# Scores one step earlier and a third buffer for gathered V in a fused block-sparse attention and MoE kernel on one Trainium2 core

## The chip, the cores and the metric

The kernel runs on one core of a Trainium2 chip. A core has five engines that run their own instruction streams and wait for one another through semaphores: TensorE (PE in the profile, with the loading of its weights shown apart as PEld), VectorE (DVE), ScalarE (ACT), GpSimd (POOL) and SyncE (SP, which here only starts transfers). Transfers go through 16 DMA engines. The metric is the device time of one launch in microseconds; smaller is better.

## The reference

Attention over 4 batches, 8 heads, 768 positions of 64 features, in 24 blocks of 32 positions, and then a mixture of experts on its output:

```python
mask = np.abs(blk_i - blk_j) <= 1
mask |= (blk_i == 0) | (blk_j == 0) | (blk_i == 23) | (blk_j == 23)
for qb in range(24):
    for kb in sampled_blocks[qb]:          # 3 blocks per query block, data
        mask[rows(qb), cols(kb)] = True
attn = softmax(where(mask, q @ k.T / 8, -1e9))
x = (attn @ v) as rows of 3072 tokens x 512

logits = x @ w_gate                        # 8 experts
e = argmax(logits); g = softmax(logits)[e]; s = sigmoid(x @ w_output_gate)[e]
out = g * s * (relu(x @ w1[e]) @ w2[e])    # w1 512x1024, w2 1024x512
```

So query blocks 0 and 23 see all keys, and every other query block sees its own block, its two neighbours, blocks 0 and 23 and three sampled ones. Which blocks those are, and which expert a token goes to, is known only at run time.

## The kernel before, in words

**Attention.** It runs in two passes (`bp` 0 and 1), each over two batches. A pass has 52 steps: 8 Dense units for the query blocks 0 and 23, then 11 pairs `i` of query blocks with four Sparse units each, in the order (head group 0, batch 0), (0, 1), (1, 0), (1, 1). Step `u0 = 52*bp + 8 + 4*i` is the first of pair `i`. A unit is scored (S, line 490), its maximum taken by DVE (mx, 497), its exponential by ACT (P, 502), transposed by PE (T, 441), copied out of PSUM (pt, by ACT in line 448 for batch 0, by DVE in 450 for batch 1), multiplied with V (O, 515 for the window's V in `vc`, 522 for the gathered V in `vt`), copied by ACT (ob, 531), and its sums taken by DVE (den, 427, and their reciprocal, 540). S of the two batches of a head group is made together, in 32 interleaved small matmuls, in the even step (`mate`).

**What sets the order.** The program is recorded step by step, and `in_order` pins every engine to the recorded order. In a step the parts of several units are recorded: `pT` of the unit two steps back (`LAGS`), `pS` of the present one, `aH` and `dL` (copies of T), `dM`, `pO` of the unit three steps back, and so on; then come the hooks of the step, pieces of other work put there with `at(step, function, ...)`.

**Rings of buffers.** In PSUM, S has four buffers, O two, and T two. The T buffers are shared with `xp`: a finished pair goes through `turn` (line 677), recorded in step `u0+3` of a later pair, in which PE transposes its x rows into a T buffer, ACT takes the high half out (xT, 679), and DVE the low half (680), for the routing (`lp`, 689 and 690, two steps later). In SBUF there are three K buffers (`kr`), three Q buffers (`qz`), two buffers for the window's V (`vc`) and two for gathered V (`vt`).

**Gathers.** `gather_v` (line 403) issues two indirect transfers on POOL, for the sampled rows of V, two steps ahead of the pair. `gather_k` copies one sampled K block, with a factor, on ACT (383), DVE (381) or POOL (385), and `window_k` (392, 393) copies the window's K on DVE.

**Experts.** Weight pieces arrive in float32 and are split into two float16 halves: ACT makes the high half (`w_h`, 924), DVE the low one (`w_l`, 930). The table `AHEAD` puts the conversions of the first nine pieces into attention's steps; its four numbers are the steps of high, low, high and low, of 512 columns each. The program of the experts begins after step 104. Their rows of x are gathered into the `qz` buffers and three more, `xb`.

Of the kernel before, what the change touches and what calls it, by code (L numbers as in the profile page):

```python
# [28 lines left out]
VW = 65  # L29
RV = 2  # L30
RK = 3
LAGD = (0, 2, 3)
# [7 lines left out]
NE = 2  # L40
# [11 lines left out]
PLAN = 6, (20,)  # L52
AHEAD = ((73, 74, 77, 78), (81, 82, 85, 86), (89, 90, 93, 94), (96, 97, 97, 98), (97, 98, 98, 99), (99, 100, 100, 101),
         (100, 101, 101, 102), (101, 102, 102, 103), (103, 104, 104, 105))
# [36 lines left out]
def tile_kernel(ctx, tc, q, k, v, sampled, wg, wcat, out):  # L91
# [69 lines left out]

    it = sp.tile([128, 128], I32, name="it")
    places = sp.tile([1, NSLOT, 3], I32, name="places")
    ri = sp.tile([128, 1], I32, name="ri")
    vi = sp.tile([128, 2, 12], I32, name="vi")
    pb = sp.tile([128, 4], I32, name="pb")
    qbi = sp.tile([128, NB, 3], I32, name="qbi")
    wi = sp.tile([128, NPAIR, 2], I32, name="wi")
    wf = sp.tile([128, NPAIR, 2], F32, name="wf")
    dup = sp.tile([128, NB, 3], F32, name="dup")  # L170

# [29 lines left out]
    def setup_dup():  # L201

        f = sp.tile([128, NB, 3], F32, name="dupf")
        nc.gpsimd.tensor_copy(f.rearrange("p a c -> p (a c)"), raw[:, :, 0])
        nc.gpsimd.memset(dup[:, :, 0:1], 0.0)
        d = sp.tile([128, NB, 2], F32, name="dupd")
        nc.gpsimd.tensor_tensor(d, f[:, :, 1:3], f[:, :, 0:1].to_broadcast([128, NB, 2]), op=ALU.subtract)
        nc.gpsimd.tensor_tensor(d, d, d, op=ALU.mult)
        nc.gpsimd.tensor_single_scalar(dup[:, :, 1:3], d, 0.5, op=ALU.is_lt)
        d = d[:, :, 0:1]  # L210
        nc.gpsimd.tensor_tensor(d, f[:, :, 1:2], f[:, :, 2:3], op=ALU.subtract)
        nc.gpsimd.tensor_tensor(d, d, d, op=ALU.mult)
        nc.gpsimd.tensor_single_scalar(d, d, 0.5, op=ALU.is_lt)
        nc.gpsimd.tensor_tensor(dup[:, :, 2:3], dup[:, :, 2:3], d, op=ALU.add)

    def setup_const():
        nc.vector.tensor_copy(pcol, ri)
        nc.vector.tensor_single_scalar(ri, ri, 31, op=ALU.bitwise_and)
        iota128 = sp.tile([128, 128], F32, name="iota128")
        nc.vector.tensor_copy(iota128, it)  # L220
# [40 lines left out]
    def setup_blocks():  # L261
        nc.vector.tensor_copy(smp, raw[0:1, :, 0])
        sf = sp.tile([128, NB, 3], F32, name="sf")
        nc.vector.tensor_copy(sf.rearrange("p a c -> p (a c)"), raw[:, :, 0])

        qbf = sp.tile([128, NB, 3], F32, name="qbf")
        nc.vector.tensor_copy(qbf, qbi)
        dd = sp.tile([128, NB, 3], F32, name="dd")
        nc.vector.tensor_sub(dd, sf, qbf)
        bad = sp.tile([128, NB, 3], F32, name="bad")  # L270
        t0 = sp.tile([128, NB, 3], F32, name="t0")
        nc.vector.tensor_single_scalar(bad, sf, 0.5, op=ALU.is_lt)
# [42 lines left out]

    kr = [ring.tile([128, 12, 256], F32, name=f"kr{i}") for i in range(RK)]
    vc = [ring.tile([128, 2, 8, VW], F32, name=f"vc{i}") for i in range(RV)]

    qz = [ring.tile([128, 512], F32, name=f"qz{n}") for n in range(RQ)]
# [80 lines left out]
    def gather_v(bp, i):  # L400
        t = ring.tile([128, 2, 2, 8, VW], F32, tag="vt", name=f"vt{bp}_{i}", bufs=RV)
        for s in range(2):
            nc.gpsimd.indirect_dma_start(  # L403
                t[:, s].rearrange("p b j w -> p (b j w)"), None, vscr[bp],
                bass.IndirectOffsetOnAxis(ap=vidx[:, i, s:s + 1], axis=0))
        vt[bp, i] = t
# [474 lines left out]

    xbuf = qz + [ring.tile([128, 512], F32, name=f"xb{i}") for i in range(3)]

    def load_x(s):
        xgs[s] = (att.tile([128, 512], F32, tag="P", name=f"xg{s}", bufs=6) if s < NE else xbuf[2 * s % 6]).bitcast(F16)
        src = xscr[0:128 * RG[GE][1]] if s < NE else xscr
        nc.gpsimd.indirect_dma_start(xgs[s], None, src, bass.IndirectOffsetOnAxis(ap=tabs[s][:, 1:2], axis=0))  # L887

    def x_t(s):
        t = att.tile([128, 512], F32, tag="P", name=f"xs{s}", bufs=6) if s < NE else xbuf[(2 * s + 1) % 6]  # L890
        t = t.bitcast(F16)
# [111 lines left out]
    def at(n, f, *a):  # L1003
        hooks.setdefault(n, []).append((f, a))

    wide = [ring.tile([128, 2, 1024], F32, tag="vt", name=f"wide{i}", bufs=RV) for i in range(2)]
    wide += [kr[2].rearrange("p a n -> p (a n)").rearrange("p (c n) -> p c n", n=1024)]
# [40 lines left out]
    for bp in range(2):  # L1050
# [6 lines left out]
        for i in range(NPAIR):  # L1057
# [3 lines left out]

            lead = 3 if bp or i > 1 else 0
            for kind, n, ns in KC[bp]:
                at(u0 - n - lead if bp or i != 1 else u0 - min(n, 5), gather_k, bp, i, kind, ns)
            at(u0 - 3 - lead, window_k, bp, i)
            at(u0 - 5 + LAGS[2] if bp or i else 6, window_v, bp, i)
            at(u0 - 5 + LAGS[2] if bp or i > 1 else (8, 12)[i], gather_v, bp, i)
        tiles = [NPAIR] + list(range(NPAIR))
# [42 lines left out]
    for m, un in enumerate(units):  # L1111
        lags = LAGD if isinstance(un, Dense) else LAGS
        le, lt, lo = lags
        d = "0" if isinstance(un, Dense) else ""
        for lag, f in ((lt, "pT"), (0, "pS"), (lt, "aH"), (0, "dM"), (lt, "dL" + d), (lo, "pO"), (lo + 1, "aO"), (lo + 1, "dD"),
                       (le, "aE" + ("0" if le else "")), (lo + 2, "fin"), (lo + 3, "fin2")):
# [147 lines left out]
```

## Time and profile before

| what | value |
|---|---|
| median of 3 runs (lowest to highest) | 623.2 us (621.53 to 624.46) |
| the profiled execution | 622.91 us, span 621.0 us |
| PE busy | 564.4 us, 91% of the span |
| PEld busy | 391.3 us, 63% |
| DVE busy | 473.8 us, 76% |
| ACT busy | 435.5 us, 70% |
| POOL busy | 260.6 us, 42% |
| q1, transfers started by hardware queues | 61004 packets, 87.84 MB, 47.9% of the 16 DMA engines' span |
| q0, transfers started by POOL's software queue | 11744 packets, 37.64 MB, 18.2% |

The span is the time from the first instruction to the last; the 1.91 us between it and the profiled execution's time lie outside. Busy time counts instructions that run, not what an engine does while it waits, starts transfers or branches. In the views of waits, `PE T L441 <- DVE den L540` reads: PE stood before a transpose into T of line 441, and what came last of the things it waited for was DVE's instruction on den in line 540. "issue" means that the profile shows nothing it waited for. In the views by window a number in brackets is a count of instructions.

### The profile page before, as it was taken

To read this page: it belongs to the slowest core of one execution; us is meant where nothing else is said; L and a number is where in the kernel's file an instruction comes from. 1 tells how busy PE (TensorE), PEld (TensorE's weight loads), DVE (VectorE), ACT (ScalarE), POOL (GpSimd) and SP (SyncE) were. 2 spreads that over 40 slices of the span, in tenths; PEclk is the share of its full clock that TensorE was granted. 3 is DMA by queue.
4 is the path that set the end of the run, shared out by engine and by line. 5 is a ranking of instruction groups with operands and counts; after the bars stand their busy time and mean duration, and the time that the engine had idled before them with its cause. 6 is when DMAs were issued, how large, how long until landed. Compare 5 with 4: busy or idle time off the path is not lost. (4 is left out here: it accounts for less than half of the span.)

```text
span 621.0 us, 22116 instructions
## 1 busy us (share of the span) xinstructions
PE 564.4 (91%) x8275; PEld 391.3 (63%) x8275; DVE 473.8 (76%) x934; ACT 435.5 (70%) x834; POOL 260.6 (42%) x324
## 2 busy tenths in 40 slices
PE   6799988989889888888979998999999999999996
PEld 4466655555556555555757776777777777777763
DVE  4587657567657567577689988899898989989891
ACT  1466657656557777677459887887888888788871
POOL 4575758765645766665332131131312122131311
PEclk8899989999889899998699999999999999999999
DMA  8986979795865866559227399359943935823491
GB/s 312 381 260 228 320 250 296 274 283 134 285 141 204 257 210 189 176 159 272 53 64 286 83 292 357 83 145 275 301 119 95 309 76 163 265 63 81 94 295 45
DMA packets 72859, 126.94 MB, mean 204 GB/s; under 512 B 38187, under 2 KB 44459, under 8 KB 72492
## 3 DMA queue, kind: packets, MB, share of 16 engines
q1 hardware_dynamic: 61004, 87.84, 47.9%
q0 software_dynamic: 11744, 37.64, 18.2%
q8 instruction: 67, 1.10, 0.7%
q14 instruction: 44, 0.36, 0.2%
HBM read 183.09 MB, written 20.49 MB: 328 GB/s over the span
## 5 line engine op out<-in xcount | busy, mean ns | idle before, releaser
L930 DVE SCALAR_TENSOR_TENSOR kr<-r,kr 128x1024 f16<-128x1024 f32 (+1 forms) x173 | 184.5, 1110 | 17.2 <-ACT kr L924 16.2
L924 ACT ACTIVATE kr<-r 128x1024 f16<-128x1024 f32 (+1 forms) x173 | 156.4, 960 | 0.8 <-DMA r<-in_wcat_dram 0.8
L941 PEld LDWEIGHTS <-kr 128*128 128x128 f16 x2004 | 125.9, 98 | 46.8 <-issue 9.2
L981 POOL DMA_INDIRECT out_dram<-yo,tab x28 | 29.7, 1059 | 213.2 <-ACT yo L978 191.1
L972 PE MATMUL y<-kr,hh 128*128 128x512 f16 x423 | 114.0, 379 | 0.4 <-DVE hh L959 0.4
L502 ACT ACTIVATE P<-S,mx 128x256 f32<-128x256 f32 x176 | 74.5, 478 | 46.1 <-DVE mx L497 42.4
L941 PE MATMUL h<-xb,kr 128*128 128x128 f16 x1344 | 93.3, 219 | 2.1 <-DMA xb<-qz 2.1
L497 DVE TENSOR_REDUCE mx<-S 128x2 f32<-128x512 f32 x88 | 59.9, 680 | 30.2 <-PE S L490 30.1
L930 DVE SCALAR_TENSOR_TENSOR ws<-r,ws 128x1024 f16<-128x1024 f32 (+1 forms) x60 | 67.8, 1167 | 8.7 <-ACT ws L924 7.1
L403 POOL DMA_INDIRECT vt<-vscr,vidx x44 | 46.8, 1063 | 55.7 <-PE O L522 45.0
L441 PE MATMUL T<-ident,P 128*128 128x128 f32 x352 | 58.7, 291 | 11.1 <-DVE den L540 6.6
L972 PEld LDWEIGHTS <-hh 128*128 128x128 f16 x594 | 50.0, 98 | 25.7 <-DVE hh L959 1.1
L490 PE MATMUL S<-kr,qz 64*32 64x256 f32 x1408 | 59.4, 400 | 4.3 <-issue 3.8
L924 ACT ACTIVATE ws<-r 128x1024 f16<-128x1024 f32 (+1 forms) x60 | 58.1, 1015 | 0.8 <-PE y L972 0.8
L941 PEld LDWEIGHTS <-ws 128*128 128x128 f16 x684 | 44.3, 100 | 16.9 <-issue 6.1
L952 ACT ACTIVATE hh<-h 128x512 f16<-128x512 f32 (+1 forms) x56 | 30.5, 545 | 33.6 <-PE h L941 31.0
L441 PEld LDWEIGHTS T<-ident,P 128*128 128x128 f32 x352 | 38.8, 145 | 18.0 <-issue 14.0
L522 PE MATMUL O<-vt,pt 128*32 128x65 f32 x1408 | 42.0, 229 | 8.6 <-issue 4.6
L515 PEld LDWEIGHTS O<-vc,pt 128*64 128x64 f32 x704 | 28.7, 140 | 31.2 <-issue 20.8
L680 DVE TENSOR_TENSOR xT<-xp,xT 128x512 f16<-128x512 f32 x24 | 16.6, 692 | 39.4 <-ACT xT L679 36.2
L972 PE MATMUL y<-ws,hh 128*128 128x512 f16 x171 | 46.0, 379 | 0.0
L515 PE MATMUL O<-vc,pt 128*64 128x65 f32 x704 | 41.1, 238 | 3.2 <-DVE den L427 1.3
(227 smaller groups left out, 931.1 us busy)
## 6 DMA issues: line engine op xcount, KB each, us to landing
r<-in_wcat_dram SPq DMA_DIRECT2D x240, 512.0 KB
vscr<-vn SPq DMA_DIRECT2D x12, 520.0 KB
qz<-in_q_dram SPq DMA_DIRECT2D x24, 256.0 KB
xscr<-xq SPq DMA_DIRECT2D x48, 128.0 KB
vc<-vscr SPq DMA_DIRECT2D x22, 260.0 KB
kn<-in_k_dram SPq DMA_DIRECT2D x2, 1536.0 KB
vs<-in_v_dram SPq DMA_DIRECT2D x6, 512.0 KB
kn<-in_k_dram SPq DMA_DIRECT2D x6, 512.0 KB
```

The costliest lines, as they stand in the source:

```text
L403: nc.gpsimd.indirect_dma_start(t[:, s].rearrange("p b j w -> p (b j w)"), None, vscr[bp], bass.IndirectOffsetOnAxis(ap=vidx[:, i, s:s + 1] ...
L441: nc.tensor.transpose(pt[:, 128 * c:128 * c + 128], p[:, 128 * c:128 * c + 128], ident)
L490: nc.tensor.matmul(u.s[64 * h2 + 32 * qi:64 * h2 + 32 * qi + 32, hp], t[p, 64 * j + 32 * qi:64 * j + 32 * qi + 32], g[p, 1 - qi:3:1 + qi, ...
L497: nc.vector.tensor_reduce(mx, self.s, axis=AX.X, op=ALU.max, negate=True)
L502: nc.scalar.activation(p[:, 256 * hp:256 * hp + 256], self.s[:, hp], AF.Exp, bias=self.mx[:, hp:hp + 1])
L515: nc.tensor.matmul(o[64 * h2:64 * h2 + 64, hp, 0:VW], w[:, col:col + 64], cv[:, b, 4 * h2 + 2 * hg + hp], start=hp == 0, stop=False)
L522: nc.tensor.matmul(o[64 * h2 + 32 * qi:64 * h2 + 32 * qi + 32, hp, 0:VW], w[:, col:col + 32], av[:, qi, b, 4 * h2 + 2 * hg + hp], start=Fa ...
L924: nc.scalar.activation(w[:, 0, r], piece(n // 8, n % 8)[:, r], AF.Copy, scale=SW)
L930: nc.vector.scalar_tensor_tensor(w[:, 1, r], piece(n // 8, n % 8)[:, r], SW, w[:, 0, r], op0=ALU.mult, op1=ALU.subtract)
L941: nc.tensor.matmul(hps[n // 4][:, 128 * j:128 * j + 128], w[:, hl, 128 * c:128 * c + 128], x[:, c // 2, xl, c % 2], start=cnt == 0, stop=c ...
L952: nc.scalar.activation(hs[g][0], hps[g][:, 0:m], AF.Relu)
L972: nc.tensor.matmul(ys[s], a[:, m], w[:, l, 512:1024], start=n % 8 == 0 and cnt == 0, stop=n % 8 == 7 and cnt == 2)
```

## The change

Four things change, and nothing else: the scores of the Sparse units are recorded one step earlier (`ls = -1`), with the K gathers and window K a step earlier too (`lead`); gathered V gets three buffers, and its gather is recorded at `u0 - 5` in place of `u0 - 2`; the low halves of the first three weight pieces in `AHEAD` move two steps later; and to have room for the third V buffer, the three extra buffers of expert rows become one tile in the ring of the V buffers, while the constants of the setup lie in a K buffer (`kr[1]`) that isn't filled yet.

```diff
+RG_V = 3
-AHEAD = ((73, 74, 77, 78), (81, 82, 85, 86), (89, 90, 93, 94), (96, 97, 97, 98), (97, 98, 98, 99), (99, 100, 100, 101),
+AHEAD = ((73, 76, 77, 80), (81, 84, 85, 88), (89, 92, 93, 96), (96, 97, 97, 98), (97, 98, 98, 99), (99, 100, 100, 101),
...
-    it = sp.tile([128, 128], I32, name="it")
-    qbi = sp.tile([128, NB, 3], I32, name="qbi")
-    dup = sp.tile([128, NB, 3], F32, name="dup")
...
-        f = sp.tile([128, NB, 3], F32, name="dupf")
+        f = early3(4)
...
     kr = [ring.tile([128, 12, 256], F32, name=f"kr{i}") for i in range(RK)]
+    cut = kr[1].rearrange("p a n -> p (a n)")
+
+    def early3(n):
+        return cut[:, 72 * n:72 * n + 72].rearrange("p (a c) -> p a c", c=3)
+
+    it = cut[:, 0:128].bitcast(I32)
+    dup = early3(11)
+    qbi = early3(12).bitcast(I32)
...
     def gather_v(bp, i):
-        t = ring.tile([128, 2, 2, 8, VW], F32, tag="vt", name=f"vt{bp}_{i}", bufs=RV)
+        t = ring.tile([128, 2, 2, 8, VW], F32, tag="vt", name=f"vt{bp}_{i}", bufs=RG_V)
...
-    xbuf = qz + [ring.tile([128, 512], F32, name=f"xb{i}") for i in range(3)]
+    xbufs = []
+
+    def xbuf(n):
+        if not xbufs:
+            xv = ring.tile([128, 4, 512], F32, tag="vt", name="xv", bufs=RG_V)
+            xbufs.extend(qz + [xv[:, i] for i in range(3)])
+        return xbufs[n % 6]
...
-    wide = [ring.tile([128, 2, 1024], F32, tag="vt", name=f"wide{i}", bufs=RV) for i in range(2)]
+    wide = [ring.tile([128, 2, 1024], F32, tag="vt", name=f"wide{i}", bufs=RG_V) for i in range(2)]
...
-            lead = 3 if bp or i > 1 else 0
+            lead = 4 if bp or i > 1 else 1 if i else 0
...
-            at(u0 - 5 + LAGS[2] if bp or i > 1 else (8, 12)[i], gather_v, bp, i)
+            at(u0 - 5 if bp or i > 1 else (8, 10)[i], gather_v, bp, i)
...
+        ls = 0 if isinstance(un, Dense) else -1
-        for lag, f in ((lt, "pT"), (0, "pS"), (lt, "aH"), (0, "dM"), (lt, "dL" + d), (lo, "pO"), (lo + 1, "aO"), (lo + 1, "dD"),
+        for lag, f in ((lt, "pT"), (ls, "pS"), (lt, "aH"), (0, "dM"), (lt, "dL" + d), (lo, "pO"), (lo + 1, "aO"), (lo + 1, "dD"),
```

In the changed file the lines of the attention and the routing stand 8 lower (441 is 449, 490 is 498, 677 is 685), those of the expert weights 14 lower (930 is 944). No engine has more or fewer instructions. How they move, at the places that the prediction speaks of:

**PE, second pass, pair 4.** The names end in pair, batch, head group: `T_1_4_1_0` is the transpose of pass 1, pair 4, batch 1, head group 0. Before, from that transpose on (the rows after these are the rest of the 32 matmuls of S, then O of batch 1):

```order
L441 MATMUL T_1_4_1_0_5283<-ident,P_4_1_0_5178 128x128 x4
L515 MATMUL O_4_0_0_5292<-vc_182,pt_1_4_0_0_5230 64x65 x4
L522 MATMUL O_4_0_0_5292<-vt_4_5000,pt_1_4_0_0_5230 32x65 x8
L677 MATMUL xp_5324<-ident,x_2_5152 128x2x64 x4
L441 MATMUL T_1_4_0_1_5331<-ident,P_4_0_1_5248 128x128 x4
L490 MATMUL S_5_0_0_5336<-kr_181,qz_184 32x256
L490 MATMUL S_5_1_0_5337<-kr_181,qz_184 32x256
```

Now, from the transpose before that one to the first matmuls of S:

```order
L449 MATMUL T_1_4_0_0_5238<-ident,P_4_0_0_5133 128x128 x4
L523 MATMUL O_3_1_1_5247<-vc_180,pt_1_3_1_1_5179 64x65 x4
L530 MATMUL O_3_1_1_5247<-vt_3_4566,pt_1_3_1_1_5179 32x65 x8
L449 MATMUL T_1_4_1_0_5279<-ident,P_4_1_0_5196 128x128 x4
L498 MATMUL S_5_0_0_5284<-kr_178,qz_181 32x256
L498 MATMUL S_5_1_0_5285<-kr_178,qz_181 32x256
```

and from the last matmul of S on:

```order
L498 MATMUL S_5_1_0_5285<-kr_178,qz_181 32x256
L523 MATMUL O_4_0_0_5306<-vc_179,pt_1_4_0_0_5243 64x65 x4
L530 MATMUL O_4_0_0_5306<-vt_4_4818,pt_1_4_0_0_5243 32x65 x8
L685 MATMUL xp_5352<-ident,x_2_5152 128x2x64 x4
L449 MATMUL T_1_4_0_1_5359<-ident,P_4_0_1_5261 128x128 x4
L523 MATMUL O_4_1_0_5370<-vc_179,pt_1_4_1_0_5304 64x65 x4
L530 MATMUL O_4_1_0_5370<-vt_4_4818,pt_1_4_1_0_5304 32x65 x8
L449 MATMUL T_1_4_1_1_5406<-ident,P_4_1_1_5320 128x128 x4
```

S of pair 5 stood behind xp and T of head group 1; it now stands ahead of O and xp, right behind T of head group 0.

**DVE, the same place.** Before, from the maximum of head group 1's first unit to that of the next pair:

```order
L497 TENSOR_REDUCE mx_4_0_1_5232<-S_4_0_1_5212 128x2
L427 TENSOR_SCALAR den_3_0_0_5126<-O_3_0_1_5163 128x2
L392 TENSOR_SCALAR kr_179<-kn_1061 128x256
L393 TENSOR_SCALAR kr_179<-kn_1061 128x768
L930 SCALAR_TENSOR_TENSOR ws_4949<-r_3611,ws_4949 128x512
L497 TENSOR_REDUCE mx_4_1_1_5288<-S_4_1_1_5213 128x2
L450 COPY pt_1_4_1_0_5290<-T_1_4_1_0_5283 128x512
L427 TENSOR_SCALAR den_3_1_0_5181<-O_3_1_1_5234 128x2
L540 RECIPROCAL den_3_0_0_5126<-den_3_0_0_5126 128x4
L680 TENSOR_TENSOR xT_5323<-xp_5324,xT_5323 128x2x256
```

Now, from window K on:

```order
L400 TENSOR_SCALAR kr_176<-kn_1075 128x256
L401 TENSOR_SCALAR kr_176<-kn_1075 128x768
L702 TENSOR_REDUCE lsum<-lp_5226 128x16
L505 TENSOR_REDUCE mx_4_0_1_5245<-S_4_0_1_5159 128x2
L435 TENSOR_SCALAR den_3_0_0_5136<-O_3_0_1_5181 128x2
L505 TENSOR_REDUCE mx_4_1_1_5302<-S_4_1_1_5160 128x2
L458 COPY pt_1_4_1_0_5304<-T_1_4_1_0_5279 128x512
L435 TENSOR_SCALAR den_3_1_0_5199<-O_3_1_1_5247 128x2
L548 RECIPROCAL den_3_0_0_5136<-den_3_0_0_5136 128x4
L688 TENSOR_TENSOR xT_5351<-xp_5352,xT_5351 128x2x256
```

Window K and the weight's low half stood between the two maxima, ahead of the copy of T; window K now stands ahead of both maxima, and the low half (not among these rows) after the xT.

**POOL, first pass, the gather for pair 10.** Before:

```order
L431 TENSOR_TENSOR x_7_3128<-ob_7_0_0_2866,den_7_0_0_2871 128x256
L658 TENSOR_TENSOR xq_3102<-x_6_2897,xq_3102 128x2x256
L431 TENSOR_TENSOR x_7_3128<-ob_7_1_0_2921,den_7_1_0_2926 128x256
L403 DMA vt_10_3226<-vscr_78,vidx 128x1040 x2
L780 DMA table<-vals,place 25600x4
```

Now:

```order
L439 TENSOR_TENSOR x_6_2897<-ob_6_1_0_2686,den_6_1_0_2691 128x256
L357 COPY vn_1141<-vs_5_2630 128x16x64
L411 DMA vt_10_3072<-vscr_78,vidx 128x1040 x2
L788 DMA table<-vals,place 25600x4
L439 TENSOR_TENSOR x_7_3117<-ob_7_0_0_2877,den_7_0_0_2882 128x256
```

The two gathers stand ahead of the x rows of pair 7, behind which they stood before; on POOL nothing else moves there.

More of the change, by code (lines that the diff above doesn't have):

```diff
@@ L201, in setup_dup @@
     def setup_dup():
-        f = sp.tile([128, NB, 3], F32, name="dupf")
+        f = early3(4)
         nc.gpsimd.tensor_copy(f.rearrange("p a c -> p (a c)"), raw[:, :, 0])
         nc.gpsimd.memset(dup[:, :, 0:1], 0.0)
-        d = sp.tile([128, NB, 2], F32, name="dupd")
+        d = early3(5)[:, :, 0:2]
         nc.gpsimd.tensor_tensor(d, f[:, :, 1:3], f[:, :, 0:1].to_broadcast([128, NB, 2]), op=ALU.subtract)
@@ L218, in setup_const @@
         nc.vector.tensor_single_scalar(ri, ri, 31, op=ALU.bitwise_and)
-        iota128 = sp.tile([128, 128], F32, name="iota128")
+        iota128 = cut[:, 128:256]
         nc.vector.tensor_copy(iota128, it)
@@ L262, in setup_blocks @@
         nc.vector.tensor_copy(smp, raw[0:1, :, 0])
-        sf = sp.tile([128, NB, 3], F32, name="sf")
+        sf = early3(6)
         nc.vector.tensor_copy(sf.rearrange("p a c -> p (a c)"), raw[:, :, 0])
-        qbf = sp.tile([128, NB, 3], F32, name="qbf")
+        qbf = early3(7)
         nc.vector.tensor_copy(qbf, qbi)
-        dd = sp.tile([128, NB, 3], F32, name="dd")
+        dd = early3(8)
         nc.vector.tensor_sub(dd, sf, qbf)
-        bad = sp.tile([128, NB, 3], F32, name="bad")
-        t0 = sp.tile([128, NB, 3], F32, name="t0")
+        bad = early3(9)
+        t0 = early3(10)
         nc.vector.tensor_single_scalar(bad, sf, 0.5, op=ALU.is_lt)
@@ L879, in load_w @@
         nc.sync.dma_start(piece(s, j), src, cond=chg)
-    xbuf = qz + [ring.tile([128, 512], F32, name=f"xb{i}") for i in range(3)]
+    xbufs = []
[4 more added lines that the diff above has]
+        return xbufs[n % 6]
     def load_x(s):
-        xgs[s] = (att.tile([128, 512], F32, tag="P", name=f"xg{s}", bufs=6) if s < NE else xbuf[2 * s % 6]).bitcast(F16)
+        xgs[s] = (att.tile([128, 512], F32, tag="P", name=f"xg{s}", bufs=6) if s < NE else xbuf(2 * s)).bitcast(F16)
         src = xscr[0:128 * RG[GE][1]] if s < NE else xscr
@@ L889, in x_t @@
     def x_t(s):
-        t = att.tile([128, 512], F32, tag="P", name=f"xs{s}", bufs=6) if s < NE else xbuf[(2 * s + 1) % 6]
+        t = att.tile([128, 512], F32, tag="P", name=f"xs{s}", bufs=6) if s < NE else xbuf(2 * s + 1)
         t = t.bitcast(F16)
```

## The prediction

> **What bounds the kernel now.** The page's first part comes first, to see which engine is near its limit over the whole span.
>
> ```profile
> PE 564.4 (91%) x8275; PEld 391.3 (63%) x8275; DVE 473.8 (76%) x934; ACT 435.5 (70%) x834; POOL 260.6 (42%) x324
> ```
>
> TensorE (PE) is busy for 91%, so at most 56.6 us of the 621.0 are its idle time; a change that leaves its instructions alone can win only from that and from a low clock. Where the idle time lies, the windows by stage tell: the middles of the two attention passes (first and third row), what joins them (second), the last routing (fourth), the experts (fifth). Behind each stretch stand its length and the busy time of PE, PEld, DVE, ACT and POOL, then granted clock, DMA share and GB/s.
>
> ```profile
> 35.91:136.83 100.92, 89.55 (x1880) 59.77 (x1879) 69.54 (x216) 65.97 (x180) 69.91 (x92) 0.98 0.85 274
> 136.83:185.43 48.60, 42.57 (x716) 27.95 (x715) 31.86 (x97) 28.52 (x76) 26.22 (x36) 0.93 0.72 195
> 185.43:278.78 93.35, 80.16 (x1715) 53.24 (x1714) 62.31 (x192) 67.43 (x183) 60.55 (x75) 0.98 0.64 199
> 278.78:326.00 47.22, 39.04 (x551) 28.68 (x551) 35.09 (x94) 26.89 (x53) 19.59 (x19) 0.82 0.47 132
> 326.00:621.00 295.00, 286.54 (x3129) 204.19 (x3126) 254.29 (x261) 234.28 (x314) 66.19 (x54) 1.00 0.62 180
> ```
>
> The experts keep PE busy for 286.54 of 295.00; the change moves nothing there but buffers, so they only shift with the attention's end. In the first and third stretch (10 and 9 query pairs) PE idles 11.37 and 13.19 us. One period of a pair, undisturbed and with a stall, in the same columns:
>
> ```profile
> 106.26:115.02 8.76, 8.24 (x189) 5.71 (x188) 6.15 (x17) 6.30 (x18) 7.00 (x9) 1.00 1.02 376
> 257.47:268.25 10.78, 9.54 (x190) 5.94 (x189) 6.29 (x17) 7.46 (x21) 7.40 (x10) 1.00 0.59 179
> ```
>
> A pair can pass in 8.76 us; the mean is 10.09 in the first stretch (100.92/10) and 10.37 in the third (93.35/9). What PE and its neighbours wait for, from the view of waits between 36 and 300 us (total, times, longest):
>
> ```profile
> PE T L441 <- DVE den L540: 6.6, 10, 1.7
> PE O L522 <- issue: 4.6, 7, 1.6
> PE O L522 <- DMA vt<-vscr,vidx: 3.9, 2, 2.7
> PE S L490 <- issue: 3.8, 6, 1.4
> PE T1d L441 <- DVE xT L680: 3.9, 2, 2.0
> POOL vt L403 <- PE O L522: 45.0, 18, 3.7
> DVE xT L680 <- ACT xT L679: 35.7, 21, 3.8
> ACT xT L679 <- PE T L441: 12.1, 11, 2.9
> ACT xT L679 <- PE xp L677: 6.6, 6, 2.8
> L441 PE MATMUL T<-ident,P 128*128 128x128 f32 x352 | 58.7, 291 | 11.1 <-DVE den L540 6.6 <-issue 2.3 <-DVE mx L497 1.3
> ```
>
> Two waits of PE can be touched by the change: 11.1 us ahead of the transposes T (the last row, from the groups by form between 40 and 300 us, holds all their releasers) and 3.9 us on gathered V. The waits ended by "issue" before S and O, and those of the Dense units (T1d), belong to work that isn't moved.
>
> **The T stall.** One of the ten, PE first, then DVE, then ACT:
>
> ```profile
> 264.91 0.66 PE L441 MATMUL T<-ident,P 128*128 128x128 f32 x4
> 265.50 0.45 PE L515 MATMUL O<-vc,pt 128*64 128x65 f32 x8
> 266.25 0.66 PE L677 MATMUL xp<-ident,x 128*128 128x128 f32 x4
> 267.69 0.63 PE L441 MATMUL T<-ident,P 128*128 128x128 f32 x4 [0.79 <-DVE den L540]
> 268.25 1.09 PE L490 MATMUL S<-kr,qz 64*32 64x256 f32 x32
> 269.27 0.45 PE L515 MATMUL O<-vc,pt 128*64 128x65 f32 x8
> 265.19 0.56 DVE L393 TENSOR_SCALAR kr<-kn 128x768 f32<-128x768 f32 x1
> 265.66 0.69 DVE L930 SCALAR_TENSOR_TENSOR ws<-r,ws 128x512 f16<-128x512 f32 x1
> 266.86 0.68 DVE L450 COPY pt<-T 128x512 f32<-128x512 f32 x1
> 269.08 0.69 DVE L680 TENSOR_TENSOR xT<-xp,xT 128x512 f16<-128x512 f32 x1 [1.39 <-ACT xT L679]
> 267.71 0.42 ACT L383 ACTIVATE kr<-kn 128x256 f32 x1
> ```
>
> T has two PSUM buffers, shared with xp. The T of 267.69 takes the buffer that the T of 264.91 filled; DVE empties it only from 266.86 to 267.54, having first done window K (L393) and the low half of a weight (L930). What PE has between these two T is O, 0.75 us (265.50 to 266.25), and xp, 0.66: not enough. The profile names den because it came last on DVE.
>
> **Scores a step sooner.** S of a pair goes between the first T and that O. Its price on PE is the same 1.02 us (268.25 to 269.27), but the cover of the DVE eviction grows from 1.41 to 2.43 us. Here T started 0.79 us late, and S alone gives 1.02. Three of the weight pieces that are converted during attention also lose their low half (0.69) from its place ahead of the eviction: it runs two steps later. I count the whole of the T stalls as gone except the part that isn't on a T buffer emptied by L450: of 11.1 I take 10, bounds 5 (only half fit in the added 1.02 and the rest move on) and 11.1. S itself needs its K sooner: the K gathers and window K move a step with it, the same number of instructions on DVE, ACT and POOL, so their slack to S stays. S has four PSUM buffers; a step sooner, it asks for those whose exponentials stood three steps back and now stand two back, still over one step of 2.2 us (8.76/4) away: nothing. Only the first pair of a pass keeps its gathers where they were, with S one step nearer: 0 to 2.2 us; I take 0, since the Dense units fill PE ahead of it.
>
> **What the cover was taken from.** xp takes the other T buffer; the T after next needs it back, after ACT's xT and then DVE's. An undisturbed case, PE and ACT, and one where xT is late:
>
> ```profile
> 105.24 0.66 PE L677 MATMUL xp<-ident,x 128*128 128x128 f32 x4
> 105.93 0.59 ACT L679 CAST xT<-xp 128x512 f16<-128x512 f32 x1 [1.02 <-PE xp L677]
> 124.63 0.38 PE L677 MATMUL xp<-ident,x 128*128 128x128 f32 x2
> 126.58 0.59 ACT L679 CAST xT<-xp 128x512 f16<-128x512 f32 x1 [1.25 <-PE T L441]
> ```
>
> Before, PE had T 0.56 (267.69 to 268.25), S 1.02 and O 0.75 between xp's end and that T: 2.33 us. Now S is gone from there: 1.31. The chain that must fit is 0.03 (105.90 to 105.93) + 0.59 + 0.69 + a handover of 0.03, or 1.34 us when ACT starts at once. So every lateness of ACT now shows on PE. In the late row it is 1.57 us (126.58 less 125.01), but eleven of these waits are recorded as ended by the T behind xp, not by xp: they go with the T stall, which leaves. What stays is ACT's own work: a K gather of 0.42 us (L383) now issues in the step of xp in the first pass as well, where ACT stood idle for 1.02. I take 0.25 us, rather more than half of it, for each of 20 pairs (the last of each pass has no S behind it): **+5 us**; bounds 0 (row of 105.93) and 1.57 x 20 = 31.
>
> **The third V buffer.** The gather of a pair writes a buffer that the pair two back still reads, so POOL stands 45.0 us in 18 waits, and the data can come late:
>
> ```profile
> 81.34 0.30 PE L522 MATMUL O<-vt,pt 128*32 128x65 f32 x2
> 84.32 0.43 PE L522 MATMUL O<-vt,pt 128*32 128x65 f32 x14 [2.69 <-DMA vt<-vscr,vidx]
> 80.74 1.35 POOL L403 DMA_INDIRECT vt<-vscr,vidx  x1 [1.49 <-PE O L522]
> 82.39 0.94 POOL L403 DMA_INDIRECT vt<-vscr,vidx  x1 [0.30 <-issue]
> 85.10:88.40 3.30, 3.30 (x43) 0.50 1.02 402
> 88.50:91.90 3.40, 3.40 (x96) 1.00 0.70 271
> ```
>
> With three buffers and the issue three steps sooner (6.6 us), the slot's last reader ends a step before the issue, so both gathers, 1.35 and 0.94 us of POOL, leave without a wait; behind them stand K gathers, x and xq, which come sooner too. **-3.9 us**, bounds 0 (if the transfer only waits elsewhere: the DMA share is 1.02 at 85 us) and -3.9. After the gap of 2.69 us the granted clock was 0.50 for 3.30 us (43 instructions, against 96 in the 3.40 after it; the columns are length, PE busy, clock, DMA share, GB/s): half of it, 1.65 us, goes as well, bounds 0 and -1.65.
>
> [...]
>
> **Buffers that change address.** Expert rows in a slot of the V ring and setup constants in a K buffer add no instruction. The slot's last gathered V is long read when the first row comes, and the constants' readers end before that K buffer is filled: 0. If that cover were gone, one wait at the start or at the experts' start, at most one period of 8.76 us.
>
> **Sum.** The profiled execution took 622.91 us, of which 621.0 is the span; the median is 623.2, 0.05% off, so no correction. 622.91 - 10 - 3.9 - 1.65 + 5 = **612.4**, forecast **612 us**. Its own range, with T between -5 and -11.1 and xT between 0 and 8 (0.4 each), is 605 to 619.
>
> **Rivals.**
> 1. The T stall only changes place: xT is late by another 0.5 us a pair, 20 x 0.5 = 10, as much as T gains. Only V and clock stay: 622.9 - 5.6 + 5 = 622 us. For it: DVE xT waited 35.7 us for ACT's, in all 21 waits. Against it: those waits were hidden, and many follow a stalled T.
> 2. Slower: ACT reaches xT late by the mean of its recorded waits, (12.1 + 6.6)/17 = 1.1 us, in every pair, and each now holds the T of step u0+5: +22 against -15.5, 629 us; with 1.57 each, 639. It decides from 15.5/20 = 0.78 us a pair. For it: ACT's step now begins with a gather. Against it: at 105.93, with T behind xp unhindered, ACT started 0.03 after xp.
> 3. Much better: every pair takes the 8.76 us of the undisturbed one: 10 x 1.33 + 9 x 1.61 = 27.8, so 595 us. For it: DVE, ACT and POOL are busy for 7.00 at most in that period. Against it: the "issue" waits (4.6 and 3.8) and the Dense units stay, and PE was busy for 9.54 in the stalled period.
> 4. The change doesn't do what it says: a scheduler might put S back. The order of the instructions shows it moved; no chance of its own.
>
> **How the numbers follow.** Forecast 0.55, rival 1 0.20, rival 2 0.13, rival 3 0.12. A difference of 0.5% (3.1 us) is about what a measurement of this kernel can tell from none. Faster is the forecast and rival 3, 0.67; the same is rival 1, 0.20; slower is rival 2, 0.13. The range goes from rival 3's 595 to just short of rival 2's 629: 595 to 628 leaves out half of rival 3, more than half of rival 2 and little else.
>
> **What would show it.** Right: no wait of T for den over 0.3 us between 36 and 300 us; POOL's wait before V under 5 us; no wait of O on a V transfer, and no clock of 0.50 near 85 us; mean periods near 9.7 us in both passes (10.2 less 10.5/20); the experts as long as before. Wrong: the transposes T waiting as long as before, now ended by DVE xT, with ACT's xT starting over 0.8 us after xp (rivals 1 and 2); or a new wait at the first pair of a pass. A longer last stretch would refute the zero for the buffers.

## The result, and the profile after

The changed kernel took 643.79 us (median of four runs, 641.56 to 648.35); the kernel before took 623.83 us on the same chip (621.53 to 624.80). The ratio is 1.0335, 95% interval 1.0267 to 1.0402. The forecast was 612 us, so even the sign was wrong here. Medians are of all runs of a kernel; ratios leave out runs in a slower state. The profiled execution took 641.56 us, 18.65 more than the one before.

The waits of the changed kernel between 36 and 300 us (total, times, longest), and from its page the groups of transposes, scores and the two halves of O (count, busy us, mean ns, idle us ahead of them and what ended it):

```profile
PE O L530 <- issue: 22.3, 39, 1.2
POOL vt L411 <- PE O L530: 30.4, 15, 3.7
ACT xT L687 <- PE xp L685: 34.4, 19, 4.3
...
L530 PE MATMUL O<-vt,pt 128*32 128x65 f32 x1408 | 51.0, 232 | 22.3 <-issue 22.3
...
L449 PE MATMUL T<-ident,P 128*128 128x128 f32 x352 | 58.3, 289 | 2.7 <-issue 1.4
...
L498 PE MATMUL S<-kr,qz 64*32 64x256 f32 x1408 | 52.5, 391 | 2.7 <-issue 1.4
...
L523 PE MATMUL O<-vc,pt 128*64 128x65 f32 x704 | 41.4, 239 | 5.8 <-DVE den L435 4.0
```

The same half of O before (from the groups by form, 40 to 300 us) and S (from the page of before), which the prediction didn't show:

```profile
L522 PE MATMUL O<-vt,pt 128*32 128x65 f32 x1408 | 42.0, 229 | 8.6 <-issue 4.6 <-DMA vt<-vscr,vidx 3.9
...
L490 PE MATMUL S<-kr,qz 64*32 64x256 f32 x1408 | 59.4, 400 | 4.3 <-issue 3.8
```

The row of T fell from 11.1 us of idle time to 2.7, and the wait for gathered V (3.9) is gone. In their place stands a wait with no releaser, 22.3 us in 39 pieces, inside the half of O that reads gathered V: with its busy time, which such pieces stretch, that group went from 50.6 to 73.3 us. S went the other way, from 63.7 to 55.2 us with its idle time. One pair, PE, then POOL and ACT:

```profile
84.31 1.09 PE L498 MATMUL S<-kr,qz 64*32 64x256 f32 x32
85.33 0.45 PE L523 MATMUL O<-vc,pt 128*64 128x65 f32 x8
85.72 0.24 PE L530 MATMUL O<-vt,pt 128*32 128x65 f32 x1
86.17 0.31 PE L530 MATMUL O<-vt,pt 128*32 128x65 f32 x3 [0.21 <-issue]
86.89 0.48 PE L530 MATMUL O<-vt,pt 128*32 128x65 f32 x12 [0.41 <-issue]
87.31 0.66 PE L685 MATMUL xp<-ident,x 128*128 128x128 f32 x4
...
84.09 1.01 POOL L411 DMA_INDIRECT vt<-vscr,vidx  x1 [0.93 <-PE O L530]
85.41 0.94 POOL L411 DMA_INDIRECT vt<-vscr,vidx  x1 [0.30 <-issue]
88.00 0.59 ACT L687 CAST xT<-xp 128x512 f16<-128x512 f32 x1 [1.02 <-PE xp L685]
```

Sixteen matmuls that take 0.4 us at a stretch are handed out in three portions over 1.6 us (85.72 to 87.31). It happens in the first O of a pair, the one between S and xp, beside POOL's two gathers, which begin as soon as the last O of the step before ends (here 0.29 us behind it, 84.09 against 83.80). Where POOL scatters to the expert table right behind the gathers, it lasts up to 3.4 us (254.77 to 258.19). In what follows a first O is beside two gathers when it begins between the start of the first and the end of the second (36 to 300 us), and broken when two of its matmuls start more than 0.3 us apart. Here 15 of 15 were broken; from their first matmul to xp they took 29.4 us more together than at the 0.75 us of an unbroken one. In six of the 15 no packet of the queues that the page calls "instruction" was on its way, so a late load of instructions isn't seen as the cause.

Where the 18.5 us of span came from, by the stretches of the prediction (same columns; here they end at the first x tile that PE turns for the experts, 325.03 us before and 339.33 now):

```profile
35.20:136.91 101.71, 88.06 (x1878) 60.15 (x1878) 67.63 (x206) 64.87 (x176) 68.79 (x92) 1.00 0.86 281
136.91:190.21 53.30, 42.98 (x719) 27.82 (x718) 35.19 (x102) 29.98 (x80) 28.61 (x38) 0.97 0.70 178
190.21:289.49 99.28, 84.66 (x1712) 57.35 (x1711) 63.26 (x187) 64.96 (x178) 58.65 (x71) 0.93 0.62 186
289.49:339.33 49.84, 37.49 (x566) 27.23 (x565) 38.85 (x108) 29.52 (x60) 19.03 (x18) 0.90 0.45 108
339.33:639.50 300.17, 290.98 (x3143) 207.16 (x3143) 254.05 (x261) 234.17 (x314) 67.24 (x54) 0.98 0.62 179
...
203.20:210.00 6.80, 6.39 (x74) 0.50 0.89 224
...
339.70:343.10 3.40, 3.40 (x27) 0.50 1.04 370
401.20:404.60 3.40, 3.40 (x16) 0.50 0.77 291
```

First pass +0.8 us, the stretch between the passes +4.7, second pass +5.9, last routing +3.6 (46.25 before, from 278.78 to 325.03), experts +4.2 (295.97 before), and the start 0.7 less. The sixth row is a stretch at half clock in the second pass. Most of the experts' share is two more of them (last two rows; half of 6.8 is 3.4 us), the first of them right behind the wait for that x tile. So 10.7 of the 18.5 us lie ahead of the last routing. In the two passes (+6.7) PE gained on T, on V and on S, and lost more in O. What the stretch between the passes and the last routing lost wasn't taken apart.

### The profile page after: what moved, and what is told of

Same layout as the page of the kernel before. It is cut to its first block, busy times and chain, and to the rows that moved or that the text cites. A ratio compares the mean times of both kernels' runs of the same rounds, so it can differ in the third digit from the quotient of the medians.

```text
span 639.5 us, 22127 instructions
## 1 busy us (share of the span) xinstructions
PE 569.5 (89%) x8275; PEld 396.1 (62%) x8275; DVE 479.3 (75%) x934; ACT 435.4 (68%) x834; POOL 260.1 (41%) x324
## 5 line engine op out<-in xcount | busy, mean ns | idle before, releaser
L944 DVE SCALAR_TENSOR_TENSOR kr<-r,kr 128x1024 f16<-128x1024 f32 (+1 forms) x173 | 184.4, 1109 | 17.3 <-ACT kr L938 15.5
L955 PE MATMUL h<-xv,kr 128*128 128x128 f16 x1344 | 94.3, 220 | 3.2 <-DMA xv<-qz 2.9
L944 DVE SCALAR_TENSOR_TENSOR ws<-r,ws 128x1024 f16<-128x1024 f32 (+1 forms) x60 | 71.8, 1233 | 9.8 <-ACT ws L938 8.3
L530 PE MATMUL O<-vt,pt 128*32 128x65 f32 x1408 | 51.0, 232 | 22.3 <-issue 22.3
L411 POOL DMA_INDIRECT vt<-vscr,vidx x44 | 43.0, 976 | 40.9 <-PE O L530 30.4
L498 PE MATMUL S<-kr,qz 64*32 64x256 f32 x1408 | 52.5, 391 | 2.7 <-issue 1.4
L966 ACT ACTIVATE hh<-h 128x512 f16<-128x512 f32 (+1 forms) x56 | 30.4, 543 | 35.2 <-PE h L955 31.5
L530 PEld LDWEIGHTS O<-vt,pt 128*32 128x32 f32 x1408 | 30.5, 112 | 34.3 <-issue 27.8
```

Source lines behind the costliest of these rows:

```text
L411: nc.gpsimd.indirect_dma_start(t[:, s].rearrange("p b j w -> p (b j w)"), None, vscr[bp], bass.IndirectOffsetOnAxis(ap=vidx[:, i, s:s + 1] ...
L498: nc.tensor.matmul(u.s[64 * h2 + 32 * qi:64 * h2 + 32 * qi + 32, hp], t[p, 64 * j + 32 * qi:64 * j + 32 * qi + 32], g[p, 1 - qi:3:1 + qi, ...
L530: nc.tensor.matmul(o[64 * h2 + 32 * qi:64 * h2 + 32 * qi + 32, hp, 0:VW], w[:, col:col + 32], av[:, qi, b, 4 * h2 + 2 * hg + hp], start=Fa ...
L944: nc.vector.scalar_tensor_tensor(w[:, 1, r], piece(n // 8, n % 8)[:, r], SW, w[:, 0, r], op0=ALU.mult, op1=ALU.subtract)
L955: nc.tensor.matmul(hps[n // 4][:, 128 * j:128 * j + 128], w[:, hl, 128 * c:128 * c + 128], x[:, c // 2, xl, c % 2], start=cnt == 0, stop=c ...
L966: nc.scalar.activation(hs[g][0], hps[g][:, 0:m], AF.Relu)
```

## The experiments

One thing must be known to read the numbers: the runs lie in seven groups, each on one chip (six of these are known to be different chips; that of the first isn't on record). The median of the kernel before is about 620 to 624 us in three groups (623.8, 619.8, 622.8) and about 613 in the other four (613.0, 613.0, 614.3, 613.0), though single runs of the two kinds overlap. Ratios are always against before on the same chip. That the two kinds differ in just this wait was found only late.

**Which part costs it.** Scores alone, in the kernel before:

```diff
-((lt, "pT"), (0, "pS"), ...
+((lt, "pT"), (0 if isinstance(un, Dense) else -1, "pS"), ...
-            lead = 3 if bp or i > 1 else 0
+            lead = 4 if bp or i > 1 else 1 if i else 0
```

> The kernel before with the scores and the K gathers one step sooner, two V buffers, V gathered at u0-2 as before. In the changed kernel no T waits for DVE any more, but the matmuls of O with gathered V stand still for 22.3 us in 39 waits with no releaser, each beginning beside POOL's second gather. Theory A (the gathers hold PE up wherever they fall, and the change moved them beside O): this kernel loses the T stalls and keeps what it has on V, so 612 to 620 us, and no new waits in O before the gathers. Theory B (the new order of PE's work is at fault: S and O stand back to back, and PE is not given its small instructions fast enough): as slow as the changed kernel, 640 us or more, with 15 to 22 us of waits inside O.

and the third V buffer with the gathers three steps sooner alone (the changed kernel with `ls = 0`, the old `lead` and the old `AHEAD`):

> The changed kernel with its third V buffer and the gathers at u0-5, but the scores, the K gathers and the weights' low halves back in their old places. Theory A: the gathers still begin as soon as the buffer's last reader ends, so PE stands still beside them too: 630 us or more, with waits of PE beside most gathers. Theory B: no new waits in O, the V waits of 3.9 us gone: 617 to 621 us.

Measured on one chip of the 620 kind: scores alone 640.26 us, ratio 1.0344 (1.0268 to 1.0420); gathers alone 621.97 us, 1.0003 (0.9950 to 1.0056). From the waits of PE (36 to 320 us), two rows of the first and two of the second, then S in the page of the second:

```profile
PE O L522 <- issue: 23.5, 46, 1.2
PE T L441 <- DVE den L540: 1.3, 1, 1.3
```

```profile
PE T L449 <- DVE den L548: 7.8, 11, 1.4
PE O L530 <- issue: 2.3, 4, 0.8
...
L498 PE MATMUL S<-kr,qz 64*32 64x256 f32 x1408 | 62.1, 383 | 5.8 <-issue 4.6
```

The whole loss comes with the scores, and so does the whole end of the T stall. As it was expected, theory B (PE isn't given its small instructions fast enough in the new order) stood, and A in its plain form (gathers cost the same wherever they fall) fell: with gathers at much the same moments and the old order, O hardly waits. But S pays there: 67.9 us with its idle time, against 63.7 in the kernel before, about as much as the wait for V had cost (3.9). In sum the third buffer neither gains nor costs.

**Are the gathers needed for it?** The changed kernel with no V gathers for pairs 3 to 8, and with copies of the same size by SP in their place, which parts the bytes that land from POOL's own instructions:

```diff
     def gather_v(bp, i):
+        if 3 <= i < 9:
+            vt[bp, i] = vt[bp, i % 3]
+            return
```

```diff
         for s in range(2):
-            nc.gpsimd.indirect_dma_start(...)
+            if 3 <= i < 9:
+                nc.sync.dma_start(t[:, s]..., vscr[bp][128 * s:128 * s + 128, :])
+            else:
+                nc.gpsimd.indirect_dma_start(...)
```

> The changed kernel; for pairs 3 to 8 of each pass V is not gathered, and O reads the V that pairs 0 to 2 of the pass (of the first pair of the pass, for its residue) have left, so this part of the attention is left out of what is right. Theory A: the waits inside O disappear for these 12 pairs, whose periods fall to about 8.8 to 9.3 us, and the time to 625 us or less. Theory B: the waits stay, and the time stays within 1% of 642 us.

> The changed kernel; for pairs 3 to 8 of each pass SP copies the same number of rows and bytes into the V buffer, from consecutive rows in place of the sampled ones, so these pairs work on other V. [...] Theory B: the waits stay.

Both kernels work on other V than the right one in these pairs. Measured, on the same chip: 631.49 and 631.18 us, one run each, against 640.26 with all gathers (scores alone) and 619.78 before: neither theory's number (625 or less, or within 1% of 642). Three periods of the first kernel beside which POOL gathers nothing, and two beside which it does; then one of each of the second:

```profile
67.53:75.60 8.07, 8.07 (x189) 5.63 (x189) 5.97 (x17) 6.46 (x19) 5.09 (x7) 1.00 0.92 273
75.60:83.84 8.24, 8.16 (x190) 5.62 (x189) 6.69 (x18) 6.36 (x19) 5.16 (x7) 1.00 0.62 190
83.84:91.91 8.07, 8.07 (x189) 5.63 (x188) 6.55 (x22) 6.75 (x18) 4.78 (x7) 1.00 0.76 234
110.31:121.19 10.88, 9.10 (x190) 6.06 (x189) 6.64 (x17) 6.25 (x18) 8.18 (x11) 1.00 0.55 176
121.19:133.73 12.54, 10.57 (x189) 6.96 (x188) 6.40 (x22) 6.18 (x16) 6.11 (x7) 0.86 0.81 235
```

```profile
67.70:76.28 8.58, 8.32 (x189) 5.77 (x188) 6.33 (x17) 7.04 (x20) 5.41 (x7) 1.00 0.86 268
113.79:126.04 12.25, 10.45 (x190) 7.20 (x189) 6.79 (x17) 6.38 (x17) 8.15 (x11) 0.86 0.64 233
```

Without POOL's gathers PE is busy to the last tenth (8.07 of 8.07), and a pair is faster than the 8.76 us of the best one before. The two rows with gathers are late pairs, which have scatters to the expert table beside them too; the early pairs of scores alone, by the starts of their first O's, take 9.5 us. Beside two gathers 4 of 4 first O's are broken in either kernel, elsewhere 1 of 14 without V transfers and 4 of 14 with SP's copies (one of these beside POOL's gathers of expert rows). So on this kind of chip both are needed, the new order and POOL's indirect transfers, and for the broken O's it is not mainly the bytes that land. What the bytes cost otherwise stays open: with copies the totals are alike, but single pairs take 8.58, 9.38 and 8.98 us. That the total stayed over 625 us fits the gathers that are left, those of 10 of the 22 pairs.

**Other moments for the gathers.** Four kernels, on a chip of the 613 kind. Pulled apart:

```diff
-            at(u0 - 5 if bp or i > 1 else (8, 10)[i], gather_v, bp, i)
+            at(u0 - 3 if bp or i > 1 else (8, 10)[i], gather_v, bp, i, (0,))
+            at(u0 - 2 if bp or i > 1 else (8, 11)[i], gather_v, bp, i, (1,))
-                        at(t0 + t5 + 1 + (4 if g < 4 ...
+                        at(t0 + t5 + 1 + (g < 4) + (4 if g < 4 ...
```

> The changed kernel with its POOL transfers pulled apart: the first V gather of a pair at u0-3, the second at u0-2, with an x row between them, and the scatters to the expert table a step later, behind K gathers. Starvation theory: from the first indirect transfer on POOL, PE still runs 85 to 90 instructions (1.7 us where S follows T) and then gets a few every 0.7 us until about 0.9 us after the last one. One transfer alone is 1.0 + 0.9 = 1.9 us, so each costs at most 0.2 us, not 1.5 to 3: waits inside O of 22.3 us fall below 8 us, and the time to 612 to 625 us. Rival (what hurts is where PE's order puts S, and the gathers only show it): 635 us or more.

the same in the old order (with `ls = 0`, the old `lead` and `AHEAD`):

> As the run with the POOL transfers pulled apart, but with the scores, the K gathers and the weights' low halves in their old places: the third V buffer and the spread transfers alone. Starvation theory: before, the wait of T for DVE falls into the time in which PE would be starved, so the two cover each other, and the T waits stay when the transfers are pulled apart: 610 to 620 us, T waits of 8 us or more. If T's waits had been starvation and not DVE, they go too: below 612 us with T waits under 4 us.

every gather issued a second time for pairs 3 to 8:

> The changed kernel; for pairs 3 to 8 of each pass every V gather is issued twice, with the same data. Starvation theory: the run of indirect transfers is 2.6 us longer for 12 pairs, and PE is starved for as much longer: periods of 11.5 to 14 us for these pairs, 20 to 31 us in all, about 665 us, in waits of 0.7 us at a time that move on to xp, T and the next O. If only the first gather or the V buffer's release matters: 650 us or less.

and both gathers at u0-2 again (`at(u0 - 5 + LAGS[2] if bp or i > 1 else (8, 12)[i], gather_v, bp, i)`), with three buffers:

> The changed kernel with three V buffers, but the gathers recorded at u0-2 again. Their buffer has been free for a step or more, so they leave when POOL comes to them, behind x rows, not at the end of an O. Starvation theory: the waits fall 85 to 90 PE instructions behind the first gather, on whatever stands there, still 1 to 3 us a pair: 630 to 645 us. If it is the coincidence with the buffer's release that hurts: 620 us or less.

Measured: apart 611.44 us, ratio 0.9977 (0.9938 to 1.0015); apart in the old order 610.21, 0.9954 (0.9920 to 0.9988); twice 738.97 (expected about 665), one run; at u0-2 608.83 against 613.04, one run. I took the first as proof that pulling apart had helped. It was none: at u0-2 POOL runs two gathers in a row again, T, O, T, S and a first O (88 matmuls) pass beside one such pair of gathers without a gap, and O waits for 6.3 us in all. These 6.3 us are 4 waits, each beside a gather or within 0.9 us behind one, so this kind of chip isn't quite free of them. The doubled gathers failed as a dose, since the second one waits for the first to land (7.16 us in one case), so the V of a pair comes late and PE waits for other things. The run in the old order shows the T stalls undiminished:

```profile
PE T L450 <- DVE den L549: 15.5, 17, 1.7
PE O L531 <- issue: 2.7, 3, 1.3
```

That speaks for the prediction's reading of them, as DVE's lateness in emptying the T buffer.

**Same moment, another instruction waits.** POOL writes one column of the new buffer twice ahead of the gathers, so that these writes wait for PE and not the gathers; or it writes the whole buffer, and the gathers come 2 us later; or the gathers stand at u0-4:

```diff
         t = ring.tile([128, 2, 2, 8, VW], F32, tag="vt", ...)
+        nc.gpsimd.memset(t[:, 0, 0, 0, 0:1], 0.0)
+        nc.gpsimd.memset(t[:, 1, 0, 0, 0:1], 0.0)
```

> The changed kernel; ahead of the two V gathers POOL writes one column of the new V buffer twice, so it is these short writes that wait for the last O of the old pair, and the gathers only follow them, at nearly the same moment as before. Wait theory (PE is held up because the gather instruction itself waits for PE): no waits inside the first O of a pair, 3% faster than the changed kernel's 1.0335 of before. Coincidence theory (what counts is that both gathers run beside T, S and the first O of a pair, so beside PE's densest stretch of small instructions): 1.3 to 2.9 us in the first O of most pairs, ratio to before 1.025 to 1.04.

> As the run with the short writes, but POOL writes the whole V buffer ahead of the gathers, which so begin about 2 us later, beside the first O, xp and T and not beside S. Coincidence theory: the waits move away from the first O's start by as much: to the end of O, to xp, T or the next O, and are smaller where PE has fewer instructions there; ratio to before 1.00 to 1.02. Wait theory: as the run with the short writes. If the waits come at a fixed PE instruction whatever the gathers do, they stay in the first O.

> The changed kernel with the V gathers one step later, at u0-4, behind POOL's K gather of that step: their buffer is free by then, so they do not begin with the end of an O. Coincidence theory: the share of gathers that fall beside the first O decides, ratio between 0.99 and 1.02. Wait theory: no waits inside O, ratio 0.985 to 1.0, as with the gathers at u0-2.

> The kernel with the gathers at u0-2 again (one look gave 608.83 against 613.04 us of before), timed in five rounds: with few waits inside the first O and few of T for DVE it should be faster than before by 0.5 to 1.5%. If the one look was luck: ratio 1.00 or more.

Measured, on another chip of the 613 kind: short writes 606.88 us against 613.04, one run; whole buffer 633.15, one run; at u0-4 608.04, ratio 0.9893 (0.9847 to 0.9938); at u0-2 609.96, 0.9887 (0.9819 to 0.9955). With the short writes and, in many pairs, at u0-4 the gathers lie as in the changed kernel, from 1.5 or 1.6 us ahead of the gathered half of the first O to 0.6 or 0.8 us behind its start; but beside two gathers 12 of 14 first O's, and 9 of 9, ran unbroken. That fits neither of the two theories. In the run with the whole buffer other waits are long: window K took DVE longer (1295 ns for the smaller copy in the mean, 717 in the run with the short writes), and S waited 9.1 us for DVE's lsum.

**The chip.** What was left in common was that every run with the new order and few such waits had been on a chip of the 613 kind. So the changed kernel, the kernel before and the short writes ran together on one more chip, and the changed kernel and the spread gathers on yet another:

> The changed kernel itself, on the chip that the next two runs share. The kernel before has taken 623.8, 619.8 and 613.0 us on the chips so far, and every run without waits inside the first O was on a chip of the 613 kind. Chip theory (the waits inside O belong to a chip or to how the program is loaded there, and the kernel runs without them elsewhere): on a 613 chip the ratio to before is 0.985 to 1.00, with under 5 us of waits inside O. Kernel theory (the waits belong to the changed kernel's order of gathers everywhere): ratio 1.025 to 1.04 with some 20 us of waits inside O.

> The kernel before, for a profile of it on this chip. Chip theory: on a 613 chip its waits ended by 'issue' before S and inside O (8.4 us on the first chip) are under 3 us, while T still waits for DVE. Kernel theory: they are as on the first chip.

> The run with two short writes ahead of the gathers, on the same chip as the changed kernel. Kernel theory: 3% faster than it, with no waits inside O. Chip theory: the same time as the changed kernel within 1%, whichever kind of chip this is.

> The changed kernel and the run with its POOL transfers pulled apart, on one more chip. On two chips where the kernel before takes about 620 to 624 us the changed kernel is 3% slower, and the short writes ahead of the gathers change nothing there (644 us); on two chips where it takes 613 us no run has waits inside O. If the kind of chip decides: on a 613 chip 0.985 to 1.00 with under 5 us of waits inside O, on a 620 chip 1.025 to 1.04 with some 20 us. If the changed kernel is slow everywhere: 1.025 to 1.04 on either.

> As the earlier run with the POOL transfers pulled apart (0.9977 on a 613 chip). If two gathers in a row beside T, S and the first O are the cause on 620 chips, pulling them apart takes most of the loss away there: 0.99 to 1.01. If any gather beside small matmuls costs the same there, wherever it stands: 1.02 or more. On a 613 chip: 0.99 to 1.00 as before.

> The run with the POOL transfers pulled apart, once more, hoping for a chip of the 620 kind, where the changed kernel is 3% slower and no version with single gathers has run. If the run of two gathers beside T, S and the first O is what costs there: ratio 0.99 to 1.01, under 8 us of waits inside O. If every gather costs the same wherever it stands: 1.02 or more, with waits of 0.7 us on O, T and S. On a 613 chip: 0.99 to 1.00 again, which leaves this open.

The first chip was of the 620 kind: changed kernel 642.52 us against 622.79, ratio 1.0314 (1.0268 to 1.0360); before 621.39, one run (with "issue" waits of 2.2 us on S and 1.9 in the gathered half of O, where the first chip had 3.8 and 4.6); short writes 644.12, one run. The second was of the 613 kind: changed kernel 606.00 against 614.29, **0.9888 (0.9798 to 0.9979)**; spread 609.30, 0.9943 (0.9904 to 0.9983). The last was also of the 613 kind: spread 611.13, 0.9973 (0.9933 to 1.0012). The changed kernel on the first of these chips, the short writes on it, and the changed kernel on the second:

```profile
PE O L530 <- issue: 23.9, 39, 1.4
```

```profile
PE O L532 <- issue: 20.1, 42, 0.6
```

```profile
PE O L523 <- DVE den L435: 7.2, 8, 1.8
PE T L449 <- DVE den L548: 3.5, 3, 1.7
PE O L530 <- issue: 3.1, 3, 1.6
...
80.32 1.09 PE L498 MATMUL S<-kr,qz 64*32 64x256 f32 x32
81.34 0.45 PE L523 MATMUL O<-vc,pt 128*64 128x65 f32 x8
81.73 0.44 PE L530 MATMUL O<-vt,pt 128*32 128x65 f32 x16
82.09 0.66 PE L685 MATMUL xp<-ident,x 128*128 128x128 f32 x4
...
80.11 1.00 POOL L411 DMA_INDIRECT vt<-vscr,vidx  x1 [1.99 <-PE O L530]
81.42 0.94 POOL L411 DMA_INDIRECT vt<-vscr,vidx  x1 [0.31 <-issue]
```

The same program, the same pair, the gathers again 1.62 us ahead of the half of O that reads them and as long as before: sixteen matmuls in one portion, 0.36 us to xp, where the chip of the first profile took 1.59. Of the first O's beside two gathers 1 of 12 was broken on this chip, 14 of 14 on the one of the 620 kind; with the short writes 15 of 15 on the chip of the 620 kind, 2 of 14 on one of the 613 kind. The mean granted clock hardly differs (0.969 here, 0.963 and 0.955 on the others). Chip theory stands, kernel theory falls as a rule for all chips. Every chip whose number is known appears in one group of runs only, so the chip itself isn't told apart from whatever else the runs of a group may share.

What this doesn't settle: why chips differ, how POOL's transfers hold up PE, and whether spreading the gathers helps on the 620 kind, since all three runs of it were on the other. Nor was a version found that beats the kernel before on both kinds. On the 613 kind the changed kernel, the gathers at u0-4 and at u0-2 are alike, 1.1% faster than before (intervals from 0.2 to 2.0%); on the 620 kind the best complete kernels are the one before and the gathers alone.

## Why the prediction was wrong

- **The T stall (-10).** The mechanism was right, the size nearly: 11.1 us went to 2.7 on the first chip (-8.4), though DVE's den now holds up the window's half of O for 4.0 us, where it was 1.3. On the 613 kind more of it stands there (10.0 us ahead of that half of O, 7.2 of it ended by den, in the page of that run).
- **V waits and clock (-3.9, -1.65).** The wait for V is gone, and the first pass has its full clock (1.00). But the half clock came back elsewhere: 6.8 us at 0.50 from 203.2 us on, and twice 3.4 us in the experts.
- **xT (+5).** Too dear: it measured nothing. No T of a Sparse unit waits for DVE's xT between 36 and 300 us, and ACT starts it 0.03 us after xp ends in the quoted row (87.31 + 0.66, then 88.00). The rivals that rested on a late xT, the slower one among them, named the wrong mechanism; that one of them pointed to a slower kernel was luck.
- **The POOL waits.** Expected under 5 us, measured 30.4: the gathers stand three steps sooner and still wait for the end of an O, since POOL runs that far ahead. That this wait costs nothing by itself is argued, not shown; it sets the gathers right behind that O.
- **Its own range.** From the bounds that the prediction gives for it (T -5 to -11.1, xT 0 to 8) it is 606 to 620, not 605 to 619. Nothing hangs on it.
- **The step that failed** is the sentence that "the waits ended by 'issue' before S and O [...] belong to work that isn't moved". They did move with the order. Before, PE had T and O beside the gathers (4 and 24 small matmuls), then xp and a T that had to wait; now S stands between T and O, and makes 60 small matmuls ahead of xp of those 28. The cost, 20 to 24 us of waits in the gathered half of O on chips of the 620 kind, stands in no term of the sum. The trace of before showed such a place, in S:

```profile
115.02 0.69 PE L490 MATMUL S<-kr,qz 64*32 64x256 f32 x11
116.08 2.21 PE L490 MATMUL S<-kr,qz 64*32 64x256 f32 x21 [0.36 <-issue]
...
114.36 0.95 POOL L403 DMA_INDIRECT vt<-vscr,vidx  x1 [0.30 <-issue]
116.12 1.04 POOL L780 DMA_INDIRECT table<-vals,place  x1 [0.17 <-issue]
```

S takes 3.2 us (115.02 to the next O at 118.22) where others take 1.02, waits for nothing, and POOL's transfers run at the same time. Most of this is in S's busy time and little in its waits; of the 3.8 us of "issue" waits on S two, 2.6 us together, end more than 4 us behind POOL's last transfer, so not beside it. To set the places of long S against POOL's transfers would have put a price beside the gain of 15.5 us, as a slower rival: 2.2 us a pair at most, or 44 for 20 pairs, an estimate from this one row.

The waits of O before (4.6 us) are weaker evidence. Two rows of one pair, and the second of them as it stands in the later profile of the kernel before on a chip of the 620 kind:

```profile
103.31 0.30 PE L522 MATMUL O<-vt,pt 128*32 128x65 f32 x2
104.88 0.43 PE L522 MATMUL O<-vt,pt 128*32 128x65 f32 x14 [1.27 <-issue]
...
106.50 0.43 PE L522 MATMUL O<-vt,pt 128*32 128x65 f32 x14 [1.30 <-DMA vt<-vscr,vidx]
```

The third matmul of this half is the first that reads the pair's second V transfer. Three of the seven waits, 3.1 us, end right there, as the wait for V at 84.32 in the prediction does, and none with the third buffer alone. So they are more likely waits for V that the profile didn't name.

On a chip that hardly has the cost the changed kernel gained about 6.9 us by the ratio (0.0112 x 614.29), where 11 were forecast. No trace of the kernel before was taken on such a chip, so which terms of the sum made this gain isn't shown.

## What to carry to other kernels

A wait with no releaser needn't belong to the work it stands before (here 22.3 us in O, beside POOL's gathers): see which transfers and engines run beside it, and price it for every place that the change moves there. Look at what its first matmul reads, too, since it can be a wait that the profile didn't name (here more likely than not 3.1 of 4.6 us). Filling PE's stall with other work can remove the stall, and with it the slack in which something else was hidden: on the first chip T's idle time fell from 11.1 to 2.7 us, and that of the gathered half of O rose from 8.6 to 22.3. A gain or loss of 1 to 3% is measured on more than one chip before it is believed: here the same program was 3.3% slower on one and 1.1% faster on another.

## What the runs showed of the hardware that was not expected

- The same program on different chips: beside POOL's two gathers the first O of a pair was broken in 15 of 15 and 14 of 14 cases in two groups of runs, in 18 of 18 in a third (with the scores alone), and in 1 of 12 in a fourth. In the quoted pair the matmuls came in portions that start at 85.72, 86.17 and 86.89 us; in the changed kernel's first profile the last portion began 0.4 to 1.0 us after POOL's last transfer instruction had ended.
- The smaller copy of window K (128x256) on DVE took 605 ns in the mean on the chip of the 613 kind where the changed kernel took 606.00 us, and 331 on the first chip, with the same program: the chip that is faster in all is the slower one here. Other kernels on chips of the 613 kind had 405 (apart, old order) to 717 (short writes), so it isn't the chip alone. In the run with POOL's writes of a whole buffer it was 1295.
- A PE gap of 2.66 us (before 339.33 us) was followed by half clock for 3.4 us in the changed kernel; one of 2.62 us at the same place in the kernel before was not (clock 1.00 there). The half clock from 203.2 us on followed no single long gap: from 200.0 to 203.2 us PE was busy for 1.77 us, in portions with waits of at most 0.52 us.
